# A q projection between two table sums, and value projections beside logits, in a fused attention and state-space kernel

## The chip, the cores and the metric

The kernel runs on one core of a Trainium2 chip. The core has five engines that run side by side and wait for one another through semaphores: TensorE (PE, matrix products, and PEld, its weight loads), VectorE (DVE), ScalarE (ACT), GpSimd (POOL) and SyncE (SP, which here only issues DMA transfers). SP and POOL each issue transfers in order from a queue of their own; the transfers run on 16 DMA engines. TensorE writes into PSUM, a small memory of eight banks, from which ScalarE or VectorE copies results into SBUF, the main on-chip memory. The metric is the device time of one execution in microseconds (us); lower is better.

## The reference

Two independent computations on inputs of 2048 positions and 640 channels, with their results side by side:

```
def _A_ref(x, wqkv, wo):                  # 32 heads of 20, W, dil = 8, 2
    qkv = (x @ wqkv) -> q, k, v
    idx = pos[:, None] - (arange(W) * dil)[None, :];  mask = idx >= 0
    logits = einsum("bhsd,bhswd->bhsw", q, k[idx]) * scale, masked
    o = einsum("bhsw,bhswd->bhsd", softmax(logits), v[idx])
    return o.reshape(B, S, D) @ wo

def _B_ref(u, A_re, A_im, B_re, B_im, C_re, C_im, log_dt, Dskip):
    P = exp(dt * A * l)                   # complex, 640 x 192 x 2048
    K = einsum("dn,dnl,dn->dl", C, P, dt * B).real
    y = irfft(rfft(pad(u)) * rfft(pad(K)))[:L]
    return y + u * Dskip
```

A is attention in which each position sees itself and seven earlier ones, two apart. B makes a convolution kernel K of length 2048 for each channel as a sum over 192 complex exponentials, and convolves the input with it by Fourier transforms of length 4096.

## The kernel before

**Part B.** The 640 channels are worked in five chunks c = 0 to 4 of 128. For a chunk, tables of exponentials and of sines are made (ScalarE) and multiplied into tables P, Q, F, G, X (`small_half`, one half h at a time) and Y (`y_form`, VectorE, line 305). A `unit(c, h, uu)` makes three Y tables and sums them against X with 192 matmuls (`kgen_unit`, lines 318 and 323; TensorE) into Ksb, which four units fill. `transform` is the forward Fourier step of K (two stages of matmuls, lines 337 and 343), `products` multiplies it with the stored transform of u (line 358), `inverse_a` is the first inverse step (line 374): four pieces of 16 matmuls, each copied into Z by ScalarE (line 375); after the fourth piece SP stores Z to Zdram. For chunks 0 to 3 this is interleaved with the next chunk's tables; for chunk 4, `LAST`, it runs beside the attention's second half.

**Part A.** The positions are taken in four strips of 512, each in a first and a second half of 256 (hf = 0, 1). `proj_k`, `proj_q` make k and q transposed, a channel tile ct at a time (10 matmuls and one copy each, lines 464 and 482). `products(hf, w)` multiplies q with k shifted by 2w (VectorE, line 521), `logits(hf, w)` sums that over the 20 channels of each head with a 0/1 matrix Gs (20 matmuls, line 531); `softmax_a`, `softmax_b` follow. The value projection `proj_v(d)` makes a pair of value rows with 40 matmuls into two PSUM banks (line 495), `proj_v1(d)` a single one with 20 into one bank (in the listings under line 420, tile ps_v); `v_halo` fills in the last 14 positions of the strip before. `av_step` multiplies values with the attention weights (VectorE, line 584, into a ring of six buffers) and sums over w on TensorE (ps_o); the positions and channels of it are worked in six groups of eight steps. `out_piece` is the output projection (ps_op).

**The second inverse step.** Class `Inverse`: Z is loaded back in four quarters (`load(qr)`, 15 transfers of 128 KB each, line 637; quarters 0 to 2 are issued before the attention-value groups, quarter 3 between them, part on SP and part on POOL). `part` works three, three or two positions at a time: 24 parts in all, six to a quarter of Z (ps_ib, 8 or 12 matmuls), copied by ScalarE into `ysb` (line 650), a ring of four buffers each of which takes three parts, and stored by SP from there (line 653). `fill(parts)` in the loops hands out the next part. So parts 0 to 5 read the first quarter, 6 to 11 the second, 12 to 17 the third; part 12 uses the ysb buffer of parts 0 to 2 again.

**What sets the order.** The program is written as one stream. A planner gives each engine a fixed order from it before the kernel runs: of the instructions that are ready by its estimates, it takes the one that stands earliest in the program. `keep_in_program_order` and `issue_after` pin some. From `att.in_order()` on, all matmuls of attention and of `part` keep program order. At run time each engine works its list strictly in order.

**Memory.** A pool hands out tiles by tag; a tag has one buffer or `bufs` in rotation, in the order of the program. Rotation sets the order in PSUM too: `big` takes the three two-bank buffers of tag "bank2" (projections of q, k, pairs of v, transform, inverse_a, ps_o), `one` the two one-bank buffers of "bank" (logits, single v, parts, output projection, and `kgen_unit`'s sums). Pool `tabb` holds the tables, laid out in the order P (3 KB a partition), F (4.5), G (6), four Y (6 each), two X (9 each), UD (2), Ksb (4). When it is closed, pool `a1` takes the same place: the pair of product buffers "prod" (20 KB), the pair "v2" (20.5 KB, over most of three Y buffers and the edge of the first X), qT1, lsb1. With `reuse_waits="tile"` a new tile waits until all work on each old tile that it lies over is done.

**Around the change.** For chunk 4 TensorE does, after the first units, `proj_k(0, 0..4)`, unit (4,1,0), unit (4,1,1), and then the five `proj_q(0, ct)` with four products behind each, the logits of the first half with `proj_k(1, ·)` between, `softmax_a(0)`, `proj_q(1, ·)`, and the loop of the second half's logits with `transform(LAST)` at w = 0, `softmax_b(0)` at 2, `products` and the four inverse pieces at 4, and value pairs at w = 1, 3, 5, 7. Eight values are made there as four pairs; the other twelve are made as singles in the first attention-value group, two before each of its first six steps, with two parts at w = 4 and two at w = 5.

Of the kernel before, what the change touches and what calls it, by code (L numbers as in the profile page):

```python
# [402 lines left out]
class Attention:  # L403
# [34 lines left out]
    def open_q0(self):  # L438
        QL = self.ta.tile([128, 9216], bf16, name="ql", tag="R0")
        self.q = [QL[:, 0:5120].rearrange("p (c s i) -> p c s i", c=5, s=4), None]  # L440
        self.lsb[0] = QL[:, 5120:9216].bitcast(f32).rearrange("p (w i) -> p w i", w=W)
        self.wv = self.ta.tile([128, 5, D], bf16, name="wv", tag="TX")
        self.nc.gpsimd.dma_start(out=self.wv[:], in_=self.wsrc[:, :, 2 * D:3 * D])

    def open_rest(self, a1):
        nc = self.nc
# [4 lines left out]
        self.Gs = a1.tile([128, 5, 32], bf16, name="Gs")  # L451
        nc.sync.dma_start(out=self.Gs[:], in_=nc.inline_tensor(gs_np.astype(ml_dtypes.bfloat16), name="c_Gs").ap())
# [55 lines left out]
    def v_halo(self, d0, nd):  # L508
# [8 lines left out]
                MM(ps[to:to + 32], lhsT=self.ident[sl, 0:32], rhs=self.ident[sl, 0:HALO].unsqueeze(1).to_broadcast([32, nd, HALO]), start=True, stop=True, tile_position=(32 * s, to), skip_group_check=True)  # L517
        self.nc.scalar.copy(out=self.v2[:, d0:d0 + nd, 0:HALO], in_=ps)

    def products(self, hf, w, c0=0, c1=5):  # L520
        self.nc.vector.tensor_tensor(out=self.prod[w % (4 - 2 * hf)][:, c0:c1], in0=self.q[hf][:, c0:c1], in1=self.kT[:, hf, c0:c1, :, HALO - DIL * w:HALO - DIL * w + 256], op=A.mult)  # L521

    def logits(self, hf, w):
        nc = self.nc
        MM = self.MM
        if w % 2 == 0:
            self.lps = self.one("ps_l")[:].rearrange("p (a b) -> p a b", a=2)
        ps, pr = self.lps, self.prod[w % (4 - 2 * hf)]
        for ct in range(5):
            for sc in range(4):  # L530
                MM(ps[32 * sc:32 * sc + 32, w % 2], lhsT=self.Gs[:, ct, :], rhs=pr[:, ct, sc, :],
                   start=(ct == 0 and w % 2 == 0), stop=(ct == 4), tile_position=(0, 32 * sc), skip_group_check=True)
        if w % 2 == 1:
            nc.scalar.activation(out=self.lsb[hf][:, w - 1:w + 1, :], in_=ps, func=ACT.Copy, scale=SCALE)
            for ww in (w - 1, w) if hf == 0 else ():
                if ww > 0:
                    nc.gpsimd.memset(self.lsb[0][0:32, ww, 0:DIL * ww], -1e9)
# [121 lines left out]
def body(tc, ctx, pools, prm, B_u, B_Dskip, Sd, Zd, UDd, A_x, A_wqkv, A_wo, out_a, out_b):  # L659
# [37 lines left out]
    def transform(c):  # L697
        Sk[c] = fwd(tc, pools, C, (lambda ut: Kb[c][:, ut, :]), 1, fp)[0]

    def unit(c, h, uu, F, G, X):  # L700
        Ys = [y_form(tc, pools, F, G, uu, k) for k in range(3)]
        kgen_unit(tc, dict(pools, psum=psg), 2 * h + uu, X, Ys, Kb[c])
        if 4 * c + 2 * h + uu in UD_AFTER:
            times_d(tc, pools, C, UDd, *divmod(UD_AFTER.index(4 * c + 2 * h + uu), 2))

    UD_AFTER = [2, 3, 5, 6, 7, 9, 10, 11, 13, 14]
    LAST = NCH - 1
    for c in range(NCH):
# [37 lines left out]
            unit(c, 1, 0, F, G, Xs[0])  # L746
        if c == 0:
            fwd_u(tc, pools, C, Sd, 1)
        unit(c, 1, 1, F, G, Xs[1])
        if c == LAST - 1:  # L750
            att.load_x()
    tabs.close()
    att.open_rest(ctx.enter_context(tc.tile_pool(name="a1", bufs=1, reuse_waits="tile")))
    for ct in range(5):
        att.proj_q(0, ct)
        for w in range(4):
            att.products(0, w, ct, ct + 1)
# [12 lines left out]
    for w in range(W):  # L770
        if w >= 2:
            att.products(1, w)
        att.logits(1, w)
        if w == 0:
            transform(LAST)
        elif w == 2:
            att.softmax_b(0)
        elif w == 4:
            P1, P2, _ = products(tc, pools, Sk[LAST], Sd[LAST], fp, False)
            for f in inverse_a(tc, pools, C, P1, P2, Zd[LAST], fp):  # L780
                f()
        if w in (1, 3, 5, 7):
            att.proj_v(w - 1)
    att.v_halo(0, 8)
    fft.close()
    att.in_order()
# [109 lines left out]
```

## Time and profile before

| what | us |
| --- | --- |
| median of 3 runs | 447.49 (445.54 to 448.25) |
| profiled execution, own time | 445.28 |
| its span | 443.5 |
| TensorE busy, share of the span | 358.7, 81% |
| VectorE busy | 392.6, 89% |
| ScalarE busy | 314.6, 71% |
| mean granted clock of TensorE | 0.915 |

The profile is one execution recorded by the hardware profiler; all its times count from the span's start. A timeline line is: start, duration, engine, line of the program, operation, output <- input with their shapes, count (x), and in brackets the idle time before it and what ended that. A line of engine times by stretch is: from and to, length, then for PE, PEld, DVE, ACT and POOL the busy time with the count, then the granted clock of TensorE (1.00 is full), the share of DMA time, and GB/s. SPq is SP's queue of DMA issues. "issue" is time in which the engine waited for nothing that the profile shows. Matmuls overlap, and their ends are modelled, so the starts are the better guide.

### The profile page before, as it was taken

What the parts mean: (1) busy time and instruction counts of PE and PEld (TensorE: products, weight loads), DVE (VectorE), ACT (ScalarE), POOL (GpSimd) and SP (SyncE); (2) the same over time, 40 slices, a digit from 0 to 9 for tenths busy, and PEclk for the clock granted to TensorE, in tenths of its full rate; (3) what the DMA queues carried; (4) which work ended last, traced back from release to release, by engine and by line L of the source; (5) the groups of instructions that cost most, each with busy time, mean ns of one, the idle gap of its engine ahead of it and who ended that gap; (6) DMA issues with size and microseconds to landing.
All of it is one profiled execution on the core that took longest, in us unless ns stands there. A gap on an engine that the chain in (4) does not pass through costs nothing.

```text
span 443.5 us, 17699 instructions
## 1 busy us (share of the span) xinstructions
PE 358.7 (81%) x8041; PEld 241.5 (54%) x8041; DVE 392.6 (89%) x394; ACT 314.6 (71%) x576; POOL 41.1 (9%) x85
## 2 busy tenths in 40 slices
PE   1385759989878987879687989899997679769896
PEld 0243656867755676457555665544556646424443
DVE  8889999999979999999999889669799989768751
ACT  3984999889998999799997815244486354635653
POOL 7440000000000000000010000000000030503110
PEclk9967888999896999699896989999999699959999
DMA  5589003171251404431299905200004097797243
GB/s 145 185 158 187 5 1 121 38 254 50 96 187 55 98 28 191 143 75 28 120 278 176 248 15 199 98 1 1 1 0 98 2 248 198 196 209 215 82 104 117
DMA packets 45131, 51.62 MB, mean 116 GB/s; under 512 B 31376, under 2 KB 38992, under 8 KB 42368
## 3 DMA queue, kind: packets, MB, share of 16 engines
q1 hardware_dynamic: 41520, 41.41, 35.5%
q0 software_dynamic: 3392, 8.95, 7.2%
q8 instruction: 63, 1.03, 1.0%
q10 hardware_dynamic: 144, 0.12, 0.1%
q14 instruction: 12, 0.10, 0.1%
HBM read 28.03 MB, written 18.35 MB: 105 GB/s over the span
## 4 chain that ended last, share of the span: by engine, by line
PE 44%; ACT 29%; DVE 11%; issue 6%; DMA 5%; SPq 4%; ACTq 0%; POOL 0%; DVEq 0%; POOLq 0%
ACT R L222 10%; ACT A L338 6%; PE ps_k L318 6%; PE ps_ph L247 6%; PE ps_k L323 6%; PE ps_op L420 6%; PE ps_k L464 5%; ACT Sg L344 4%; DVE prod L521 4%; PE ps_ph L250 4%; SPq L637 3%; PE ps_ia L374 3%; DMA Z<-Zdram 3%; PE ps_o L420 3%; PE ps_f L343 2%
## 5 line engine op out<-in xcount | busy, mean ns | idle before, releaser
L305 DVE TENSOR_TENSOR Y<-F,G 128x3072 bf16<-128x3072 bf16 x60 | 103.2, 1759 | 0.4 <-PE ps_k L323 0.3
L222 ACT ACTIVATE R<-LPC 128x192 bf16<-128x192 f32 x225 | 59.3, 359 | 0.1
L247 PE MATMUL ps_ph<-LPC 128*128 128x256 bf16 (+1 forms) x200 | 41.0, 308 | 20.5 <-DMA LPC<-lo 8.0
L318 PE MATMUL ps_k<-Y,X 128*32 128x64 bf16 x1920 | 47.0, 239 | 8.3 <-issue 4.5
L323 PE MATMUL ps_k<-Y,X 64*32 64x64 bf16 x1920 | 43.2, 234 | 2.9 <-issue 2.9
L318 PEld LDWEIGHTS <-X 128*32 128x32 bf16 x1920 | 32.1, 117 | 18.1 <-issue 9.7
L344 ACT CAST Sg<-ps_f 128x1024 bf16<-128x1024 f32 x40 | 37.6, 1025 | 5.8 <-PE ps_f L343 5.8
L338 ACT CAST A<-ps_f 128x1024 bf16<-128x1024 f32 x40 | 37.6, 1032 | 1.6 <-PE ps_f L337 1.4
L584 DVE TENSOR_TENSOR prod<-v,atp 128x2048 bf16<-128x2048 bf16 (+2 forms) x32 | 31.3, 1021 | 8.3 <-PE ps_o L420 5.6
L255 ACT ACTIVATE TX<-ps_ph 128x864 bf16<-128x864 int16 (+1 forms) x40 | 32.3, 864 | 8.2 <-DVE X L271 3.9
L271 DVE TENSOR_TENSOR X<-R,TX 128x1536 bf16<-128x1536 bf16 x40 | 36.5, 958 | 0.0
L343 PE MATMUL ps_f<-A,T 128*128 128x128 bf16 x320 | 23.9, 236 | 14.9 <-ACT A L338 13.5
L323 PEld LDWEIGHTS <-X 64*32 64x32 bf16 x1920 | 29.5, 113 | 11.4 <-issue 4.2
L255 ACT ACTIVATE TA<-ps_ph 128x768 bf16<-128x768 int16 x40 | 30.4, 822 | 2.7 <-PE ps_ph L250 2.4
L247 PEld LDWEIGHTS <-LPC 128*128 128x128 bf16 x200 | 15.1, 102 | 29.0 <-issue 14.1
L343 PEld LDWEIGHTS <-T 128*128 128x128 bf16 x320 | 21.9, 106 | 16.5 <-issue 15.5
L521 DVE TENSOR_TENSOR prod<-ql,kT 128x1024 bf16<-128x1024 bf16 (+1 forms) x24 | 23.1, 1039 | 8.3 <-ACT ql L483 8.3
L250 PE MATMUL ps_ph<-LPC 128*64 128x128 bf16 (+1 forms) x400 | 29.6, 248 | 0.0
L420 PE MATMUL ps_op<-wo,o 128*128 128x320 bf16 x160 | 28.1, 312 | 0.8 <-ACT o L594 0.4
L610 ACT CAST ob<-ps_op 128x320 bf16<-128x320 f32 x28 | 11.9, 431 | 22.1 <-PE ps_op L420 20.4
L375 ACT CAST Z<-ps_ia 128x1024 bf16<-128x1024 f32 x20 | 19.3, 1014 | 11.5 <-PE ps_ia L374 11.5
L374 PE MATMUL ps_ia<-EA,P 128*128 128x128 bf16 x320 | 24.1, 238 | 3.2 <-DVE P L358 3.2
(133 smaller groups left out, 658.8 us busy)
## 6 DMA issues: line engine op xcount, KB each, us to landing
Sdram<-Sg SPq DMA_DIRECT2D x5, 1024.0 KB
P<-Sdram SPq DMA_DIRECT2D x5, 1024.0 KB
P<-Sdram SPq DMA_DIRECT2D x10, 512.0 KB
Zdram<-Z SPq DMA_DIRECT2D x5, 1024.0 KB
Z<-Zdram SPq DMA_DIRECT2D x30, 128.0 KB
U<-in_B_u_dram SPq DMA_DIRECT2D x4, 640.0 KB
UDdram<-UD SPq DMA_DIRECT2D x10, 256.0 KB
out_dram<-ysb SPq DMA_DIRECT2D x32, 80.0 KB
```

Of the source, the lines that this page charges most:

```text
L222: nc.scalar.activation(out=R[:, :, e, :], in_=src, func=ACT.Exp, scale=m)
L247: MM(o[:, :, 0:32], lhsT=L[:, 0:128], rhs=rhs, start=first, stop=last, skip_group_check=True)
L250: MM(o[64 * hh:64 * hh + 64, :, 32:48], lhsT=L[:, 128:192], rhs=rhs[:, :, 16 * hh:16 * hh + 16], start=False, stop=last, skip_group_check= ...
L255: last = nc.scalar.activation(out=dst[:, qs, e0:e0 + 2 * n, :].rearrange("p q (b e) f -> p b e q f", b=2), in_=words.rearrange("p b (e q f ...
L305: nc.vector.tensor_tensor(out=Y[:].rearrange("p q (b a) f -> p q b a f", a=8), in0=fa, in1=gb, op=A.mult)
L318: MM(ps[32 * g:32 * g + 32, t], lhsT=X[:, q, 2 - k, :, f], rhs=Ys[k][:, q, :, f], start=(t == 0 and k == 0), stop=False, tile_position=(0, ...
L323: MM(ps[32 * g:32 * g + 32, t], lhsT=X[hb, q, 2 - k, :, f], rhs=Ys[k][hb, q, :, f], start=False, stop=(k == 2), tile_position=(64 * (g // ...
L338: nc.scalar.copy(out=A1[:, :, 32 * b:32 * b + 32].rearrange("p k (j g) -> p k j g", g=4), in_=ps[:].rearrange("p j k g -> p k j g"))
L343: last = MM(ps[:, kk], lhsT=C["T2"][:, 8 * b + kk, :], rhs=A1[:, 8 * b + kk, :], start=(kk % 4 == 0), stop=True, skip_group_check=True)
L344: nc.scalar.copy(out=Sg[:, :, 8 * b:8 * b + 8, :], in_=ps[:].rearrange("p k (j g) -> p j k g", g=4))
L420: self.MM = lambda *a, **k: self.tc.keep_in_program_order(self.nc.tensor.matmul(*a, **k))
L521: self.nc.vector.tensor_tensor(out=self.prod[w % (4 - 2 * hf)][:, c0:c1], in0=self.q[hf][:, c0:c1], in1=self.kT[:, hf, c0:c1, :, HALO - DI ...
```

## The change

It has three parts.

- The five `proj_q(0, ct)` move into the last unit: after its three Y tables and before its 192 matmuls (`between`). Behind each, VectorE does the products of w = 0 and 1 for this ct alone (`first_products`). Since pool `a1` is not open yet, these ten small products get tiles of `tabb` by tags that are free: P, UD, Ksb, F, G, and one Y. The logits of w = 0 and 1 then follow the unit, before `tabb` is closed. Products 2 to 7 come as whole ones in the loop, and `proj_k(1, ·)` at w = 2 to 6. Gs, which these logits need, moves from `a1` into the tile of wv, and its load with it.
- Six value pairs instead of four are made beside the second half's logits: at w = 1, 2, 3, 4, 5 and 7. The inverse pieces of the last chunk move from w = 4 to behind the pairs of w = 5 (one), behind w = 6 (one) and behind the pair of w = 7 (two).
- The first attention-value group has eight single values instead of twelve, two before each of its first four steps; halos move one step earlier, and parts are handed out as 1, 2, 1, 1 at w = 4, 5, 6, 7 in place of 2, 2 at w = 4, 5.

```diff
-        self.wv = self.ta.tile([128, 5, D], bf16, name="wv", tag="TX")
-        self.nc.gpsimd.dma_start(out=self.wv[:], in_=self.wsrc[:, :, 2 * D:3 * D])
+        WG = self.ta.tile([128, 5 * D + 160], bf16, name="wv", tag="TX")
+        self.wv = WG[:, 0:5 * D].rearrange("p (k c) -> p k c", k=5)
+        self.Gs = WG[:, 5 * D:].rearrange("p (c h) -> p c h", c=5)
+        self.nc.gpsimd.dma_start(out=self.wv, in_=self.wsrc[:, :, 2 * D:3 * D])
...
+    def open_first(self, tabb):
+        tile = lambda n, tag, **k: tabb.tile([128, n, 4, 256], bf16, name="prod0", tag=tag, **k)
+        P, U, K, F, G, Y = tile(1, "P"), tile(1, "UD"), tile(2, "Ksb"), tile(2, "F"), tile(3, "G"), tile(1, "Y", bufs=4)
+        self.first = [[P[:, 0], K[:, 0], F[:, 0], G[:, 0], G[:, 2]], [U[:, 0], K[:, 1], F[:, 1], G[:, 1], Y[:, 0]]]
...
+    def first_products(self, w, ct):
+        self.nc.vector.tensor_tensor(out=self.first[w][ct], in0=self.q[0][:, ct], in1=self.kT[:, 0, ct, :, HALO - DIL * w:HALO - DIL * w + 256], op=A.mult)
...
-    def unit(c, h, uu, F, G, X):
+    def unit(c, h, uu, F, G, X, between=lambda: None):
         Ys = [y_form(tc, pools, F, G, uu, k) for k in range(3)]
+        between()
         kgen_unit(tc, dict(pools, psum=psg), 2 * h + uu, X, Ys, Kb[c])
...
+    def q_first():
+        att.open_first(pools["tabb"])
+        for ct in range(5):
+            att.proj_q(0, ct)
+            for w in range(2):
+                att.first_products(w, ct)
...
-        unit(c, 1, 1, F, G, Xs[1])
+        unit(c, 1, 1, F, G, Xs[1], q_first if c == LAST else lambda: None)
         if c == LAST - 1:
             att.load_x()
+    for w in range(2):
+        att.logits(0, w)
     tabs.close()
     att.open_rest(ctx.enter_context(tc.tile_pool(name="a1", bufs=1, reuse_waits="tile")))
-    for ct in range(5):
-        att.proj_q(0, ct)
-        for w in range(4):
-            att.products(0, w, ct, ct + 1)
-    for w in range(W):
-        if w >= 4:
-            att.products(0, w)
-        att.logits(0, w)
-        if w < 5:
-            att.proj_k(1, w)
+    for w in range(2, W):
+        att.products(0, w)
+        if w < 7:
+            att.proj_k(1, w - 2)
+        att.logits(0, w)
...
-            for f in inverse_a(tc, pools, C, P1, P2, Zd[LAST], fp):
+            ia = inverse_a(tc, pools, C, P1, P2, Zd[LAST], fp)
+        if w > 0 and w != 6:
+            att.proj_v((0, 0, 2, 4, 6, 8, 0, 10)[w])
+        if w >= 5:
+            for f in ia[w - 5:w - 4] if w < 7 else ia[2:]:
                 f()
-        if w in (1, 3, 5, 7):
-            att.proj_v(w - 1)
...
     for w in range(W):
-        if w < 6:
-            att.proj_v1(8 + 2 * w)
-            att.proj_v1(9 + 2 * w)
-            if w in (4, 5):
+        if w < 4:
+            att.proj_v1(12 + 2 * w)
+            att.proj_v1(13 + 2 * w)
+        if w in (3, 4, 5):
+            if w > 3:
                 fill(parts)
-                att.v_halo(*((8, 8) if w == 4 else (16, 4)))
+            if w < 5:
+                att.v_halo(*((8, 8) if w == 3 else (16, 4)))
+            else:
                 fill(parts)
+        if w > 5:
+            fill(parts)
```

More of the change, by code (lines that the diff above doesn't have):

```diff
@@ L441, in open_q0 @@
         self.lsb[0] = QL[:, 5120:9216].bitcast(f32).rearrange("p (w i) -> p w i", w=W)
-        self.wv = self.ta.tile([128, 5, D], bf16, name="wv", tag="TX")
-        self.nc.gpsimd.dma_start(out=self.wv[:], in_=self.wsrc[:, :, 2 * D:3 * D])
-    def open_rest(self, a1):
-        nc = self.nc
+        WG = self.ta.tile([128, 5 * D + 160], bf16, name="wv", tag="TX")
+        self.wv = WG[:, 0:5 * D].rearrange("p (k c) -> p k c", k=5)
+        self.Gs = WG[:, 5 * D:].rearrange("p (c h) -> p c h", c=5)
+        self.nc.gpsimd.dma_start(out=self.wv, in_=self.wsrc[:, :, 2 * D:3 * D])
         gs_np = np.zeros((128, 5, 32), np.float32)
@@ L450, in open_rest @@
                 gs_np[p, ct, (128 * ct + p) // DH] = 1.0
-        self.Gs = a1.tile([128, 5, 32], bf16, name="Gs")
-        nc.sync.dma_start(out=self.Gs[:], in_=nc.inline_tensor(gs_np.astype(ml_dtypes.bfloat16), name="c_Gs").ap())
+        self.nc.sync.dma_start(out=self.Gs, in_=self.nc.inline_tensor(gs_np.astype(ml_dtypes.bfloat16), name="c_Gs").ap())
+    def open_first(self, tabb):
+        tile = lambda n, tag, **k: tabb.tile([128, n, 4, 256], bf16, name="prod0", tag=tag, **k)
+        P, U, K, F, G, Y = tile(1, "P"), tile(1, "UD"), tile(2, "Ksb"), tile(2, "F"), tile(3, "G"), tile(1, "Y", bufs=4)
+        self.first = [[P[:, 0], K[:, 0], F[:, 0], G[:, 0], G[:, 2]], [U[:, 0], K[:, 1], F[:, 1], G[:, 1], Y[:, 0]]]
+    def open_rest(self, a1):
         pairs = [a1.tile([128, 2, 5, 4, 256], bf16, name="prod", tag=t) for t in ("prod", "v2")]
@@ L527, in logits @@
             self.lps = self.one("ps_l")[:].rearrange("p (a b) -> p a b", a=2)
-        ps, pr = self.lps, self.prod[w % (4 - 2 * hf)]
+        ps = self.lps
+        pr = self.first[w] if hf == 0 and w < 2 else [self.prod[w % (4 - 2 * hf)][:, ct] for ct in range(5)]
         for ct in range(5):
             for sc in range(4):
-                MM(ps[32 * sc:32 * sc + 32, w % 2], lhsT=self.Gs[:, ct, :], rhs=pr[:, ct, sc, :],
+                MM(ps[32 * sc:32 * sc + 32, w % 2], lhsT=self.Gs[:, ct, :], rhs=pr[ct][:, sc, :],
                    start=(ct == 0 and w % 2 == 0), stop=(ct == 4), tile_position=(0, 32 * sc), skip_group_check=True)
```

## The prediction

> **What bounds the kernel now.** I read the page first (span and busy shares), then the timelines of VectorE and TensorE from 255 us on, then SP's queue, the clock by stretch, and the DMA rate of 356 to 396 us in forty slices.
>
> ```profile
> span 443.5 us, 17699 instructions
> ...
> PE 358.7 (81%) x8041; PEld 241.5 (54%) x8041; DVE 392.6 (89%) x394; ACT 314.6 (71%) x576; POOL 41.1 (9%) x85
> ```
>
> No engine is full, so each stage has its own limit. VectorE's own gaps, in its timeline:
>
> ```profile
> 275.27 8.65 DVE L305 TENSOR_TENSOR Y<-F,G 128x3072 bf16<-128x3072 bf16 x5
> 292.23 23.07 DVE L521 TENSOR_TENSOR prod<-ql,kT 128x1024 bf16<-128x1024 bf16 x24 [8.31 <-ACT ql L483]
> 317.77 1.23 DVE L541 TENSOR_TENSOR tree<-ql 128x1024 f32<-128x1024 f32 x1 [2.46 <-POOL ql L537]
> ...
> 381.31 3.56 DVE L584 TENSOR_TENSOR prod<-v,atp 128x1536 bf16<-128x1536 bf16 x4 [2.70 <-ACT v L506]
> ```
>
> The 8.31 us before the first product is the gap that the q move aims at; the 2.70 us wait for values is what the pair move aims at. Between 317.8 and 357.3 VectorE waits only 1.7 us in all: that stage is its own. TensorE:
>
> ```profile
> 283.11 0.22 PE L318 MATMUL ps_k<-Y,X 128*32 128x64 bf16 x1 [0.98 <-issue]
> ...
> 286.83 0.23 PE L318 MATMUL ps_k<-Y,X 128*32 128x64 bf16 x1 [1.13 <-issue]
> ...
> 288.77 10.96 PE L482 MATMUL ps_q<-xT,wkq 128*128 128x512 bf16 x50
> ...
> 343.87 0.73 PE L531 MATMUL ps_l<-prod,Gs 128*32 128x256 bf16 x20 [2.19 <-DVE prod L521]
> ...
> 348.28 5.45 PE L374 MATMUL ps_ia<-EA,P 128*128 128x128 bf16 x61 [1.70 <-DVE P L358]
> ...
> 395.28 0.53 PE L420 MATMUL ps_o<-prod,ident 32*32 32x384 bf16 x10 [3.49 <-issue]
> ```
>
> From 268 to 328 us TensorE hardly pauses, so there an order change gives nothing by itself; from 341.3 to 348.3 it is busy 1.6 of 7 us; at 391.8 it stops 3.5 us in mid-step. The DMA rate, one figure per us from 356 to 396, and SP's queue:
>
> ```profile
> GB/s 369 434 299 258 207 234 249 214 231 208 227 217 232 226 195 84 175 206 204 210 192 188 24 193 200 208 160 278 207 241 232 203 224 239 222 268 190 261 224 264
> ```
> ```profile
> 386.52 0.77 SPq L637 DMA_DIRECT2D Z<-UDdram  x1
> 387.59 9.08 SPq L653 DMA_DIRECT2D out_dram<-ysb  x8
> ```
>
> The loads of Z fill this stretch: the last one of the third quarter is issued at 386.52 and, by the completion records of its semaphore, is in at 395.9. Behind it wait the first ysb stores.
>
> **q between the two units.** Before: k projection to 279.1, two units of 4.8 us each (192 matmuls at 19 ns are 3.65, plus the 0.98 and 1.13 pauses), q 10.9, products 292.2 to 315.3. After: unit, q from 283.9 to 294.8, unit to 299.7 (I keep its pause; without it 1.1 earlier), then the first two logits, 0.66 each, to 301.0. VectorE does the ten small products (20 of the same form took 12.1) behind the copies of q, done by about 297. There it stops: the new pair tile "v2" lies over three of the four Y buffers, two read by the last unit and one holding a first product, and a tile in this pool waits for every reader of each tile it covers. So products 2 to 7 start at 301.0, six at 2.75 (four took 11.0): 317.5 against 315.3, a loss of 2.2. What is behind that wait on VectorE: all six products and the softmax tree. Against it: TensorE is free of k by 301.0 + 5 x 2.92 (the period of k plus logits at 304 to 313) = 315.6 and can begin the second q, so VectorE fills part of the 2.46 gap with two small products (1.2), and the 0.75 that it later waited for a logits behind the inverse step goes. 2.2 - 1.2 - 0.75 is +0.3; I take 0 at VectorE's last product (357.3), with bounds -1.2 (no pause in the unit) and +2.2 (nothing fills).
>
> The Gs load moves to SP's queue behind the TX readers (272.9, where POOL's wv load was released too); its successor, the load of P, was issued at 273.65: nothing.
>
> **Value pairs.** Pairs 4 and 6 (2.2 us each) leave 354 to 360 for the 5.4 us of idle TensorE before the inverse step; four single values of pairs 8 and 10 (1.1 each) leave the attention-value stage. The inverse pieces then run beside two pairs instead of alone; the Zdram store stays within 1 us of 354.8. SP's first Z load is held by VectorE's last product, so the stream starts where it did.
>
> **Attention-value group one.** VectorE's work from 358.7 to 378.6 has no gap. With values there it starts at 357.3 and ends at 377.2; the next group starts 4.1 earlier than 381.31. TensorE has 8 single values instead of 12 and paces nothing.
>
> **What is late next.** This decides the sum. Group one hands out 1 + 2 + 1 + 1 = 5 parts, before 2 + 2 = 4; with 8 in group two the thirteenth, part 12, now stands at its end, before group three, on an engine kept in program order. Part 12 needs the third quarter of Z and overwrites the first ysb buffer, whose stores sit on SP behind all 38 loads. Before, it ran at 416, 20 us after its data. Also wv is free at about 366 (eight singles at 1.14 from 357) instead of 380.4, so POOL issues the four wo loads and its six of the fourth quarter then, into the same 16 engines. Bytes are unchanged; only idle DMA time can be won. Slices 15 to 26 of the row above average 157 GB/s, the later ones 230: 12 x 73/230 = 3.8 us. So the third quarter lands at 395.9 - 3.8 = 392.1 (388.5 if POOL's six, 0.56 each, do not get in front; 395.9 if nothing is won). TensorE, ready at about 387 to 389, does part 12 in 0.59 and the first step in 0.54 (the half-clock rows of 387 to 391): 393.2 against 395.74, -2.5. ScalarE's copy of part 12 waits for the stores, near 394; the other PSUM buffer covers that. The last group has one part fewer: -0.3.
>
> **Sum:** 0 - 2.5 - 0.3 = -2.8 us. The profiled execution took 445.28 (span 443.5 and 1.8 around it): 442.5. On the median of the runs shown, 447.49, that is 444.7.
>
> **Clock.** The rows:
>
> ```profile
> 345.40:352.20 6.80, 4.42 (x40) 4.17 (x41) 6.80 (x4) 1.52 (x2) 0.00 (x0) 0.50 0.00 0
> ...
> 386.40:393.20 6.80, 5.19 (x128) 1.90 (x128) 6.80 (x9) 4.01 (x8) 0.55 (x1) 0.50 1.07 226
> ```
>
> After the idle stretch the granted clock is 0.50 and 61 inverse matmuls take 89 ns each, where 34 at 266 us took 61; after the thin work of 380 to 386 it is 0.50 again up to 400. The Trainium skill, "TensorE: Matmul & The Clock Gate", section "Part 1: The HAM clock gate", says that an idle window of about 3.4 us halves the clock and a busy one restores it. By that rule the pairs keep the inverse step at full clock (64 x 28 ns = 1.8 us earlier, off the path here), but group one gets thinner and group two stays at half clock: the rule speaks against pricing group two at full clock, and in rival 1 I do not.
>
> **Rivals.** *1, the Z loads do not hold TensorE* (0.25). They land while group two still runs, as the 20 us of slack before would suggest. Then group two takes its 8.7 us (382.6 to 391.3, half clock) from 378.2, group three starts at 386.9, and the 3.49 pause, whose instruction page was fetched in the full DMA stretch, falls away: up to -8.4 - 0.3. With the quarter in at 388.5 it is -6. I take -6.5: 441.0. Against: the issue pace of SP.
>
> *2, no net gain* (0.20). The wo loads moved to 366 halve SP's stream just when the second quarter is due, and the third lands at 395.9 as before. In the row, loads that landed 0.56 apart alone landed 1.2 apart beside wo. The Trainium skill, "DMA: Bandwidth & Descriptors", section "Queues, rings and completion order", states that an engine takes turns between queues by packet, and the 1.2 agrees. Step one of group three is then done at 395.9 + 0.59 + 0.54 = 397.0, +1.3; less 0.3 that is 448.5.
>
> *3, slower* (0.15): value pairs in front of logits. TensorE's order is fixed beforehand; its 5.4 free us before the inverse step shrink to 1. The second half has two product buffers, so a pair that stands before a logits holds VectorE's product after next by up to 2.2, and everything behind 357 moves with it, SP's first load too. One such wait cancels most of the gain; from two on (4.4) the kernel is slower, with three 447.5 - 2.8 + 6.6 = 451.3. Against: logits go first when ready, and a VectorE product is 2.75 long against 0.66 + 2.2 of TensorE.
>
> **How the numbers follow.** Forecast 0.40 at 444.7. Range 440 to 450.5: rival 1 down to -7.5, rival 3 up to two waits; what is left out is the far end of both. More than 1% (4.5 us) is about what a measurement here tells from no change. Faster by that: rival 1 and the forecast's lower tail (quarter at 388.5 with the start at -1.2), 0.25 + 0.08. Slower by that: 0.12, rival 3 less its single wait. Within: 0.55.
>
> **What would show it.** Right: VectorE's gap near 297 to 301 released by TensorE's logits; product 7 of the first half ending near 317.5; last product near 357; no wait for values near 377; wo issues near 366; a stop of TensorE before part 12, released by a Z load. Wrong: an earlier start of products 2 to 7, waits of VectorE on ps_l between 328 and 357, or group three running at 387.

## The result and the profile after

The changed kernel takes 453.27 us (median of 4 runs, 450.96 to 456.94) against 447.87 for the kernel before on the same chip: a ratio of 1.0132, interval 1.0088 to 1.0176. Predicted were 444.7 and a gain of 2.8 us; by the ratio it is a loss of 5.9. The profiled execution took 453.39, 8.1 us more than that of before.

The page after, span and busy times:

```profile
span 451.6 us, 17688 instructions
...
PE 367.4 (81%) x8041; PEld 245.4 (54%) x8041; DVE 392.6 (87%) x386; ACT 315.2 (70%) x574; POOL 45.4 (10%) x85
```

VectorE does the same 392.6 us as before in a span that is 8.1 us longer, so the loss is waiting. VectorE's timeline (start, busy, engine, line, operation, count, idle ahead of it and what ended it) shows where:

```profile
300.76 16.50 DVE L530 TENSOR_TENSOR prod<-ql,kT 128x5120 bf16<-128x5120 bf16 x6 [3.38 <-PE ps_l L541]
...
349.10 8.29 DVE L530 TENSOR_TENSOR prod<-qT,kT 128x5120 bf16<-128x5120 bf16 x3
...
394.51 1.96 DVE L594 TENSOR_TENSOR prod<-v,atp 128x1536 bf16<-128x1536 bf16 x2 [5.23 <-PE ps_o L420]
```

Up to the last product (349.10 + 8.29 = 357.39; before 357.27) nothing is lost. At 394.5 VectorE waits 5.2 us for TensorE. TensorE's timeline, first the stretch of the inverse step, then the three places where it stands in the attention-value groups:

```profile
351.97 1.26 PE L541 MATMUL ps_l<-prod,wv 128*32 128x256 bf16 x20 [3.95 <-DVE prod L530]
...
354.44 2.10 PE L374 MATMUL ps_ia<-EA,P 128*128 128x128 bf16 x18
356.47 1.26 PE L541 MATMUL ps_l<-prod,wv 128*32 128x256 bf16 x20
357.66 1.09 PE L374 MATMUL ps_ia<-EA,P 128*128 128x128 bf16 x14
...
361.55 1.96 PE L374 MATMUL ps_ia<-EA,P 128*128 128x128 bf16 x32
...
380.79 0.59 PE L420 MATMUL ps_ib<-Z,HB 96*32 96x160 bf16 x12 [4.39 <-DMA Z<-Zdram]
...
393.33 0.59 PE L420 MATMUL ps_ib<-Z,HB 96*32 96x160 bf16 x12 [5.12 <-DMA Z<-Zdram]
...
401.98 0.59 PE L420 MATMUL ps_ib<-Z,HB 96*32 96x160 bf16 x12 [2.87 <-DMA out_dram<-ysb]
```

Two things are to be seen here. The four inverse pieces, which before ran in one go from 346.1 to 353.7, now stand between logits and value pairs in TensorE's fixed order and end at 363.5. And parts 0, 6 and 12, the first parts of the three quarters of Z, each wait for loads: 12.4 us in all, where before only a pause of 3.49 us stood there, in which TensorE waited for nothing that the profile shows. For part 12 the profile names a store, but the last load of its quarter was in at 401.85, 0.13 us ahead of the start. All five kernels that hand out five parts (the changed one and, below, e1, e3, e6 and e10) have the same 0.13 us between this load and part 12, and in e10 the profile names the load itself, so I read it as a wait for the load. The first output projection of group three starts at 402.98 instead of 395.74. What follows it takes 48.6 us, before 47.8.

The loads come late from their beginning. SP's queue and POOL's queue after, from 356 us on:

```profile
357.45 1.25 SPq L647 DMA_DIRECT2D Z<-Zdram  x2
358.75 0.58 SPq L647 DMA_DIRECT2D Z<-UDdram  x1
359.38 0.54 SPq L647 DMA_DIRECT2D Z<-Zdram  x1
364.61 0.34 SPq L377 DMA_DIRECT2D Zdram<-Z  x1
```
```profile
364.11 1.13 POOL L647 DMA_DIRECT2D Z<-Zdram  x2 [45.22 <-PE ps_h L523]
```

SP starts at 357.45 as forecast (357.34 before), but after four loads it stands 4.7 us behind the Zdram store, which goes out 9.8 us later than before. The store and POOL's first load of the first quarter were these lines before:

```profile
354.82 0.33 SPq L377 DMA_DIRECT2D Zdram<-Z  x1
...
354.33 1.13 POOL L637 DMA_DIRECT2D Z<-Zdram  x2 [36.59 <-ACT Z L375]
```

so this load too is 9.8 us late. In between the DMA engines are mostly idle. The two kernels' rows by stretch, before and then after (from and to, length, busy us and count of TensorE, its weight loads, VectorE, ScalarE and GpSimd, then granted clock, DMA share, GB/s):

```profile
356.00:360.00 4.00, 3.77 (x92) 2.73 (x84) 2.51 (x3) 1.61 (x2) 1.66 (x4) 1.00 0.95 340
360.00:364.00 4.00, 2.75 (x48) 1.66 (x45) 3.93 (x4) 1.71 (x3) 0.56 (x1) 1.00 1.06 226
364.00:368.00 4.00, 2.45 (x55) 2.12 (x55) 4.00 (x5) 3.02 (x4) 0.00 (x0) 1.00 1.11 221
```
```profile
356.00:360.00 4.00, 4.00 (x75) 2.90 (x76) 2.52 (x2) 2.02 (x2) 0.00 (x0) 0.75 0.20 58
360.00:364.00 4.00, 4.00 (x77) 3.12 (x73) 2.89 (x4) 2.93 (x4) 0.00 (x0) 1.00 0.26 78
364.00:368.00 4.00, 2.46 (x56) 1.55 (x49) 4.00 (x4) 2.90 (x4) 3.32 (x6) 1.00 0.67 236
```

In these 12 us (340 + 226 + 221) x 4 = 3148 kB moved before, 1488 after. From 368 to 392 us the changed kernel moves 219 to 244 GB/s with the DMA share above 1: the engines are full, and the missing 1660 kB are 7.1 us of transfer at 235 GB/s. In bytes, part of that is made up: the rows from 356 to 392 us add up to 7956 kB before and 7056 after. But wo and POOL's share of the fourth quarter, which go out 4.6 us earlier here (376.33 against 380.95), take part in that; of the Z loads, 20 are in 28.3 us behind P (below) before and 6 after, and 40 us behind P it is 36 and 23.

### The profile page after: what moved, and what is told of

It reads as the page before. It is cut to its first block, busy times and chain, and to the rows that moved or that the text cites. A ratio compares the mean times of both kernels' runs of the same rounds, so it can differ in the third digit from the quotient of the medians.

```text
span 451.6 us, 17688 instructions
## 1 busy us (share of the span) xinstructions
PE 367.4 (81%) x8041; PEld 245.4 (54%) x8041; DVE 392.6 (87%) x386; ACT 315.2 (70%) x574; POOL 45.4 (10%) x85
## 4 chain that ended last, share of the span: by engine, by line
PE 45%; ACT 29%; DVE 9%; DMA 7%; issue 6%; SPq 4%; DVEq 0%; ACTq 0%
ACT R L222 10%; ACT A L338 6%; PE ps_k L318 6%; PE ps_ph L247 6%; PE ps_k L323 6%; PE ps_op L420 6%; DMA Z<-UDdram 4%; PE ps_ph L250 4%; ACT Sg L344 4%; PE ps_q L488 4%; PE ps_f L343 3%; SPq L647 3%; DVE prod L530 3%; ACT Z L375 3%; PE ps_k L470 2%
## 5 line engine op out<-in xcount | busy, mean ns | idle before, releaser
L247 PE MATMUL ps_ph<-LPC 128*128 128x256 bf16 (+1 forms) x200 | 42.6, 317 | 16.0 <-DMA LPC<-lo 8.5
L343 PE MATMUL ps_f<-A,T 128*128 128x128 bf16 x320 | 27.1, 258 | 14.3 <-ACT A L338 13.6
L343 PEld LDWEIGHTS <-T 128*128 128x128 bf16 x320 | 25.3, 119 | 15.6 <-issue 14.3
L250 PE MATMUL ps_ph<-LPC 128*64 128x128 bf16 (+1 forms) x400 | 30.6, 255 | 0.0
L250 PEld LDWEIGHTS <-LPC 128*64 128x64 bf16 x400 | 15.6, 120 | 19.8 <-issue 19.6
L337 PE MATMUL ps_f<-BD,U 128*64 128x128 bf16 x320 | 19.4, 285 | 6.9 <-ACT Z L375 3.4
L358 DVE TENSOR_TENSOR P<-P,Sg 128x4096 bf16<-128x4096 bf16 x10 | 22.8, 2284 | 2.4 <-ACT TA L255 1.4
```

Source lines behind the costliest of these rows:

```text
L247: MM(o[:, :, 0:32], lhsT=L[:, 0:128], rhs=rhs, start=first, stop=last, skip_group_check=True)
L250: MM(o[64 * hh:64 * hh + 64, :, 32:48], lhsT=L[:, 128:192], rhs=rhs[:, :, 16 * hh:16 * hh + 16], start=False, stop=last, skip_group_check= ...
L343: last = MM(ps[:, kk], lhsT=C["T2"][:, 8 * b + kk, :], rhs=A1[:, 8 * b + kk, :], start=(kk % 4 == 0), stop=True, skip_group_check=True)
```

## The experiments

Below, P is the start of VectorE's two P products (343.74 before, 344.69 after); times from P leave out what happened earlier in an execution. "Loads in" counts the Z loads complete 28.3 us behind P, by their completion records. Ratios are against the kernel before, run beside each group, and rest on 4 to 10 executions of a kernel; the two right columns are of the one traced execution, which is long for e7 (450.22, median 444.36) and short for e5 (449.03, median 450.85).

| kernel | ratio, 95% interval | loads in | P to first output projection |
|---|---|---|---|
| before | 1 | 20 | 52.0 |
| changed | 1.0132 [1.0088, 1.0176] | 6 | 58.3 |
| e1 | 1.0028 [0.9995, 1.0060] | 18 | 53.4 |
| e2 | 1.0050 [1.0011, 1.0089] | 17 | 53.8 |
| e3 | 1.0102 [1.0060, 1.0143] | 9 | 57.1 |
| e4 | 1.0008 [0.9970, 1.0047] | 13 | 52.7 |
| e5 | 1.0112 [1.0067, 1.0157] | 10 | 53.6 |
| e6 | 1.0042 [1.0007, 1.0077] | 17 | 52.0 |
| e7 | 0.9941 [0.9904, 0.9979] | 20 | 50.8 |
| e8 | 0.9992 [0.9956, 1.0029] | 17 | 50.7 |
| e9 | 0.9928 [0.9880, 0.9975] | 17 | 49.1 |
| e12 | 0.9920 [0.9878, 0.9962] | 20 | 47.4 |
| e13 | 1.0039 [0.9998, 1.0080] | 8 | 56.1 |
| e14 | 1.0027 [0.9994, 1.0060] | 14 | 53.9 |

**Splitting the change.** First the inverse pieces back in their place, then each half of the change alone, then the late pieces alone.

```diff
 # e1, against the changed kernel
-            ia = inverse_a(tc, pools, C, P1, P2, Zd[LAST], fp)
+            for f in inverse_a(tc, pools, C, P1, P2, Zd[LAST], fp):
+                f()
         if w > 0 and w != 6:
             att.proj_v((0, 0, 2, 4, 6, 8, 0, 10)[w])
-        if w >= 5:
-            for f in ia[w - 5:w - 4] if w < 7 else ia[2:]:
-                f()
```

> The changed kernel with all four pieces of the last inverse step handed to the planner together again, right behind their two products and ahead of the fourth value pair, as the kernel before does; q between the units, the six pairs and the new placing of the parts stay. Theory A, the late Zdram store: in the changed kernel the pieces stood behind value pairs and logits in TensorE's fixed order, the store went out at 364.6 us instead of 354.8, and all Z loads behind it came late. Then here the store is issued at 355 +- 1.5, the first quarter of Z is in by 370 (changed kernel: 380), TensorE's stops before parts 0 and 6 (4.4 and 5.1 us) are gone, group three starts 5 to 8 us earlier than its 403, and the time is 445 to 448. Theory B, the thirteenth part: part 12 at the end of group two waits for the first ysb buffer's stores behind all loads on SP; its stop of about 3 us stays and the time stays above 449.5. Theory C, the q move: the time stays at 452 to 454, since q is unchanged here.

Measured: 448.85 against 447.49. Of the loss of 1.3%, 1.0% is gone, and the stops before parts 0 and 6 with it (0.3 and none). The stop before part 12 is not, as theory B had it: TensorE waits 5.52 us there, and the time is just above the 445 to 448 of theory A. So the late pieces carry most of the loss, and what is left, 1.3 us above the kernel before (by the interval -0.2 to +2.7) where 2.8 below was forecast, has other causes.

```diff
 # e2, against the kernel before; open_first, first_products, q_first, Gs and logits as in the change
-        unit(c, 1, 1, F, G, Xs[1])
+        unit(c, 1, 1, F, G, Xs[1], q_first if c == LAST else lambda: None)
...
+    for w in range(2):
+        att.logits(0, w)
     tabs.close()
...
-    for w in range(W):
-        if w >= 4:
-            att.products(0, w)
+    for w in range(2, W):
+        att.products(0, w)
+        if w < 7:
+            att.proj_k(1, w - 2)
         att.logits(0, w)
-        if w < 5:
-            att.proj_k(1, w)
```

> The kernel before with only q's first half between the two units (with its first products and logits); value pairs, inverse pieces and parts as before. Theory A (the late store): the time of the kernel before, 446 to 449, and the store at 355 +- 1; VectorE's last product stays near 357.3. Theory B (the thirteenth part): the same. Theory C (the q move costs): 451 to 454.

Measured: 449.46, +0.5%. Not free, and not the 451 to 454 of theory C. VectorE's timeline of e2, the wait for the first logits and the one ahead of its last product:

```profile
303.62 16.50 DVE L530 TENSOR_TENSOR prod<-ql,kT 128x5120 bf16<-128x5120 bf16 x6 [3.36 <-PE ps_l L541]
...
359.01 2.82 DVE L530 TENSOR_TENSOR prod<-qT,kT 128x5120 bf16<-128x5120 bf16 x1 [1.50 <-PE ps_l L541]
```

From the start of the last matmuls of k's projection to P it is 65.7 us here and 64.9 before, +0.8; and the wait ahead of the last product is 1.50 instead of 0.75, since the whole inverse step still stands before that product's logits. Together 1.6, near the 2.0 measured.

```diff
 # e3, against the kernel before: the edit of e4, below, group one of the change, and
-        if w in (1, 3, 5, 7):
-            att.proj_v(w - 1)
+        if w > 0 and w != 6:
+            att.proj_v((0, 0, 2, 4, 6, 8, 0, 10)[w])
 # e4, against the kernel before
-            for f in inverse_a(tc, pools, C, P1, P2, Zd[LAST], fp):
-                f()
+            ia = inverse_a(tc, pools, C, P1, P2, Zd[LAST], fp)
         if w in (1, 3, 5, 7):
             att.proj_v(w - 1)
+        if w >= 5:
+            for f in ia[w - 5:w - 4] if w < 7 else ia[2:]:
+                f()
```

> The kernel before with only the second half of the change: six value pairs, the pieces of the inverse step spread over the last three logits, and the new placing of the parts; q as before. Theory A (the late store): the store at 362 to 366, Z loads late, 451.5 to 454.5. Theory B (the thirteenth part): the same time, but with a stop of 3 us or more at part 12 and a first quarter that does not hold TensorE. Theory C (the q move): 446 to 449.

> The kernel before with one edit: the four pieces of the inverse step are handed over one at a time behind the fifth, one behind the sixth and two behind the last logits, as in the changed kernel. Four value pairs, parts and q as before. Theory A (the late store alone costs it): the store is issued at 360 to 364 instead of 354.8 and the time rises by 0.6 us for each us of that, as in the changed kernel (5.8 for 9.8): 450.5 to 453. Theory B or C: the time of the kernel before, 446.5 to 449, since parts and q are untouched. If the late store costs only together with six pairs, which free VectorE for group two earlier, it is between: 448.5 to 450.5.

Measured: e3 452.87 with the store 19.1 us behind P, as theory A had it (before 11.1, changed 19.9); e4 448.57, no loss, with the store 15.0 behind P. The planner's order explains the difference: with four pairs the pieces end 4 us later than before, with six 8. Four cost nothing, since the loads of the first quarter had some 5 us to spare ahead of part 0, which was this line before:

```profile
376.25 0.38 PE L420 MATMUL ps_ib<-Z,HB 96*32 96x160 bf16 x12
```

By their completion records, taken in the program's order, the last of them was in at 371.1 or a little earlier before, and in e4 at 374.47, 1 us ahead of part 0 at 375.44. In the changed kernel it was in at 380.65, 36.0 us behind P instead of 27.4, and part 0 stood 4.39 us for it. The rate of 0.6 us per us that I had put in e4's expectation was wrong: it is slack first, then a wait.

**Part 12 and the order of the inverse step.**

```diff
 # e5: the changed kernel with four parts in group one (e7 and e8 have this too)
-        if w > 5:
+        if w == 7:
             fill(parts)
 # e6: the kernel before with six pairs, group one of the changed kernel, and
         elif w == 4:
             P1, P2, _ = products(tc, pools, Sk[LAST], Sd[LAST], fp, False)
             for f in inverse_a(tc, pools, C, P1, P2, Zd[LAST], fp):
                 f()
-        if w in (1, 3, 5, 7):
-            att.proj_v(w - 1)
+        if w > 0 and w != 4:
+            att.proj_v((0, 0, 2, 4, 0, 6, 8, 10)[w])
 # e7: e6 with four parts in group one;  e8: e7 with q between the units
```

> The changed kernel with one edit: the attention-value group one hands out four parts of the out-projection of the inverse step instead of five (none at its seventh step), so that part 12 leaves group two. Theory B (part 12 holds TensorE at the end of group two): its stop of 2.9 us goes, group three starts 2 to 3 us earlier and the time is 450 to 451.5. Theory A (the late store, the loads of the first two quarters): the stops before parts 0 and 6 stay (4.4 and 5.1 us) and the time falls by no more than 1 us from 453.3: 452.3 to 454.

> The kernel before with six value pairs, but the inverse step as before: pairs 0, 2 and 4 behind the second, third and fourth logits, then the four pieces together behind their products, then pair 6 behind the sixth logits and 8 and 10 behind the last two; the parts of the changed kernel (five in group one); q as before. Theory A+B: the store is at 355 +- 1.5 and the first two quarters hold nothing; logits six is not behind a pair, so VectorE's last product does not wait more than 1 us; but the wo loads, which come 4 us earlier, take the engines' time in front of the third quarter, which is in at 395 to 397, and part 12 at the end of group two stops TensorE for 3 to 6 us: 446.5 to 449.5. Theory A alone (nothing but the order of the inverse step): 443 to 446.

> The same as the run before it with four parts in group one, so that part 12 is not in group two but comes after group three, as in the kernel before. Theory A+B: no stop at the end of group two; it ends 3 to 4 us earlier than in the kernel before: 443 to 445.5. If part 12's wait only passes to the next thing that is late (wo for the first output projection, or half-clock thin work in group two): 446 to 448.

> The same as the run before it with q's first half between the last two units, as in the changed kernel: the change with both repairs. Theory C2, from the run with q alone (+2 us): VectorE's wait of 3.4 us for the first two logits costs 1 to 2 us here too, 445 to 447.5. If what q alone cost was only noise of the units' pauses: as the run before, within 0.7 us.

Measured: e5 450.85 (+1.1%), e6 449.06 (+0.4%), e7 444.36 (-0.6%), e8 445.73 (-0.1%), against 446.48. In e5 part 12's stop is gone, those before parts 0 and 6 stay (4.09 and 5.17), and the ratio falls by only 0.2%. What part 12 costs behind a late stream is not settled by that: the two intervals allow a fall of up to 0.8%, the median of 450.85 lies in theory B's range and the ratio in theory A's, and in the traces the first output projection comes 4.7 us earlier behind P. Where the stream is in time part 12 decides the sign: e6 and e7 differ in that part alone, and in 1.0%. TensorE in e6:

```profile
394.71 0.74 PE L420 MATMUL ps_ib<-Z,HB 96*32 96x160 bf16 x12 [5.31 <-DMA out_dram<-ysb]
```

Part 12's own input, the third quarter, is in at 394.58, the same 0.13 us earlier; the profile names a store that ended about then. e8 repeats the price of q beside e7: +0.5%.

**What about the late pieces costs time?** Theory A said the late store. So e9 keeps e7's order on TensorE and holds only the store; e13 holds the memory under the first quarter of Z as well.

```diff
 # e9, against e7: the store leaves inverse_a's last piece and is issued here
     att.v_halo(0, 8)
+    nc.scalar.copy(out=held[0][:, 127, 31:32], in_=att.v2[:, 0, 0:1])
+    held[1]()            # the Zdram store; held[0] is the tile Z it reads
 # e13, against e9: three more copies between these two lines
+    for t in (P1[:, 31, 31, 3:4], P2[:, 31, 31, 3:4], EA[:, 1, 127:128]):
+        nc.scalar.copy(out=held[0][:, 127, 31:32], in_=t)
```

> The kernel of e7_v_order_p4 (q as before, six pairs, the inverse step in its old place, four parts in group one) with one thing added: the Zdram store is held back by the data. It is issued behind the halo copies of the values, and a copy of one element of v into the last column of Z makes it wait for them (so one column of the last inverse step is overwritten). TensorE's order stays as in e7. Theory A (the late store costs it by the Z stream alone): the store goes out 18 to 20 us after VectorE's P products begin (e7: 10.8; the changed kernel: 19.9), TensorE stops before parts 0 and 6 as in the changed kernel, and the time is 4 to 6 us above e7's: 448.5 to 450.5. Theory A2 (the fixed order of TensorE costs it, with logits and softmax behind the pieces, and the stream has slack): within 1.5 us of e7, 444 to 446.

> The kernel of e9_late_store with the memory under the first quarter of Z held as well: behind the copy that holds the store, three more one-column copies read the last elements of P1, P2 and EA into the same column of Z, so that the tile of the first quarter, which lies over them, is free only after the halo copies (again one column of the last inverse step is overwritten). TensorE's order is that of e7 and e9. Theory E (in the changed kernel the loads of the first quarter were held by the memory that the late inverse pieces read; 5 loads were in by 368 us against 12 in the kernel before): POOL's six loads go out 18 to 20 us after the P products begin (e9: 10.2, changed kernel: 19.4), the stops before parts 0 and 6 come to 3 to 5 us each, and the time is 3 to 6 us above e9's: 447.5 to 450. Theory A2 (TensorE's own order, with the softmax behind it, costs it): within 1 us of e9, 443.5 to 445.5.

Measured: e9 444.10 against 447.44, -0.7%, level with e7, although its store goes out 19.3 us behind P, nearly as late as in the changed kernel. Theory A falls: the store's lateness alone costs nothing there. What e9 does not test is a long stand of SP: it has six loads ahead of the store and stands 1.65 us behind it, the changed kernel four loads and 4.7 us (e5 2.5, e13 2.7, with losses of the same size). e13 449.82 against 447.85, +0.4%: 1.1% above e9, with POOL's loads 21.7 us behind P instead of 10.2 (19.4 in the changed kernel). TensorE in e9 and in e13, at parts 0 and 6:

```profile
378.37 0.39 PE L421 MATMUL ps_ib<-Z,HB 96*32 96x160 bf16 x12 [1.14 <-DMA Z<-Zdram]
...
385.26 0.59 PE L421 MATMUL ps_ib<-Z,HB 96*32 96x160 bf16 x12 [0.49 <-DMA Z<-UDdram]
```
```profile
383.12 0.59 PE L421 MATMUL ps_ib<-Z,HB 96*32 96x160 bf16 x12 [7.10 <-DMA Z<-Zdram]
...
393.71 0.59 PE L421 MATMUL ps_ib<-Z,HB 96*32 96x160 bf16 x12 [2.85 <-DMA Z<-UDdram]
```

and the first two stretches of the DMA, again e9, then e13:

```profile
356.00:360.00 4.00, 4.00 (x100) 3.00 (x94) 3.29 (x3) 2.51 (x4) 3.32 (x6) 1.00 0.46 122
360.00:364.00 4.00, 4.00 (x88) 2.64 (x80) 2.02 (x2) 1.51 (x2) 0.00 (x0) 1.00 0.74 199
```
```profile
356.00:360.00 4.00, 4.00 (x90) 2.84 (x85) 3.41 (x2) 1.21 (x2) 0.00 (x0) 1.00 0.08 21
360.00:364.00 4.00, 4.00 (x88) 2.75 (x81) 2.17 (x3) 2.59 (x4) 0.00 (x0) 1.00 0.55 167
```

POOL's first loads in the two:

```profile
356.45 1.13 POOL L638 DMA_DIRECT2D Z<-Zdram  x2 [36.18 <-DVE prod L522]
```
```profile
365.64 1.13 POOL L638 DMA_DIRECT2D Z<-Zdram  x2 [47.74 <-PE ps_v L421]
```

In e9 POOL's six loads of the first quarter go out from 356.45 on, 0.60 us after the last matmul of the pieces; in e13 from 365.64 on, 0.29 us after the last of the added copies, which ends at 365.35. The 0.60 us is the same in the kernel before, the changed kernel and e1 to e12, wherever the pieces end (from 353.64 in e12 to 363.51 in the changed kernel); the names that the profile gives for these waits change from run to run, the distance does not. That is theory E: the first quarter's tile lies over what the inverse step reads, and the loads of Z that need nothing of this step (all of the first quarter's 15 but the two that read the last chunk's Zdram) are held by it all the same. In e13 TensorE's order is that of e9, so the order itself is not needed for a loss of this kind and size. Some 3.8 us of what e13's trace has more than e9's lie behind the first output projection (50.6 us to the end, 46.8 in e9), where nothing was edited.

The reverse test takes the loads out from under the late pieces, by exchanging two buffers:

```diff
 # e14, against e5; e15 does the same to e12
-        pool, tag = ((self.a2, "Z"), (self.att.ta, "LPC"), (self.att.a1, "prod"), (self.att.ta, "U"))[qr]
+        pool, tag = ((self.att.ta, "LPC"), (self.a2, "Z"), (self.att.a1, "prod"), (self.att.ta, "U"))[qr]
```

> The kernel of e5_a_p4 (the changed kernel with four parts in group one, inverse pieces late) with the buffers of the first and second quarter of Z exchanged: the first quarter goes into the long free buffer, the second into the one that lies over the inverse step's tiles. Theory E: the first quarter's loads, but for the three of the last chunk, go out before the pieces end, on SP and POOL from 358 on; the stop before part 0 shrinks from 4.1 to under 1.5 us and the stop before part 6 by 2 or more, and the time falls from 450.9 to 446 to 448.5. Theory A2: within 1 us of e5, 450 to 452.

> The kernel of e12_pair_first (the fastest so far, q as before, inverse pieces in their old place) with the same exchange of buffers. Theory E: the first quarter's loads were not held there and nothing waits for them, so no more than 1 us either way: 442.5 to 444.5.

Measured: e14 449.05, +0.3%, 0.8% under e5 by the ratios. Its trace supports only half of it. The first quarter is free of the hold: POOL's first load goes out 4.3 us before the pieces end, and the stop before part 0 is gone (0.38). But part 6 now waits 10.76 us for the second quarter, which took over the held memory; and SP stands 5.6 us at a load that waits for the store's landing. 40 us behind P, 24 loads are in, as in e5, and the first output projection is not earlier. Exchanging buffers moves the hold, so this run does not settle theory E from its side. The time lies between what the two theories had. e15 is 0.7% under the kernel before (444.81 against 447.85), level with e12 and 0.3 us above the expected range.

**The wo loads and a pair in front of a logits.**

```diff
 # e10, against e6, and e11, against e7
-            nc.gpsimd.dma_start(out=self.wo[32 * dd:32 * dd + 32], in_=wsrc[dd])
+            nc.sync.dma_start(out=self.wo[32 * dd:32 * dd + 32], in_=wsrc[dd])
 # e12, against e7
-        if w > 0 and w != 4:
-            att.proj_v((0, 0, 2, 4, 0, 6, 8, 10)[w])
+        if w > 0 and w != 6:
+            att.proj_v((0, 0, 2, 4, 6, 8, 0, 10)[w])
```

> The kernel of e6_v_order (part 12 at the end of group two) with the four wo loads on SP's queue behind the loads of the first three quarters of Z, instead of on POOL's queue, where they go out as soon as wv is free. Theory D (wo and POOL's part of the fourth quarter share the DMA engines with the third quarter, which is why it was in no earlier): the third quarter is in 2 to 3 us earlier, part 12's stop of 5.3 us shrinks by that, and the time falls from 449.1 to 446 to 447.5. If POOL's loads of the fourth quarter, which then go out earlier still, take wo's place: 448 to 449.5. If wo comes too late for the first output projection in group three: a new stop before ps_op and 449 or more.

> The same edit of the wo loads on the kernel of e7_v_order_p4, where part 12 comes after group three and nothing in group two waits for the third quarter. Theory D: no gain there, since no part waits: within 1 us of e7's 444.4, or up to 2 us above it if the output projection waits for wo.

> The kernel of e7_v_order_p4 with the fourth value pair ahead of the sixth logits again (handed over behind the fifth, as the changed kernel does), so that TensorE's order is inverse step, pair, logits. The price of one pair in front of a logits, by the prediction up to 2.2 us: VectorE's last product waits 2 to 3.5 us for that logits instead of 0.5 to 1.5, and the time is 1.5 to 2.5 us above e7's: 446 to 447. If the slack behind it takes the wait: within 0.7 us of e7.

Measured: e10 446.56 against 447.44 (0.9970, 0.9925 to 1.0015), 0.7% under e6; e11 445.44 (0.9939), level with e7; e12 443.45 (0.9920). With wo behind the third quarter, that quarter is in 48.3 us behind P in e11 and 48.8 in e10, against 50.7 in e6 and 52.1 in e7: theory D holds for its 2 to 4 us, and in e10, where part 12 waits for that quarter, it shows in the time. In e11 TensorE then waits 5.47 us for wo ahead of the output projection, and nothing is won. In e12 VectorE's last product does wait longer:

```profile
356.56 2.83 DVE L521 TENSOR_TENSOR prod<-qT,kT 128x5120 bf16<-128x5120 bf16 x1 [2.41 <-PE ps_l L531]
```

2.41 us, in e7 0.43, but the softmax behind it starts 16.7 us after P in e12 and 16.8 in e7, because e7 has a pair between the last two logits instead. A pair must stand somewhere; before which of these two logits made no difference. e12, the changed kernel's six pairs with q and inverse step as before and part 12 out of group two, is the fastest version: 0.8% under the kernel before (0.4 to 1.2).

## Why the prediction was wrong

**The step that failed** is "the Zdram store stays within 1 us of 354.8. SP's first Z load is held by VectorE's last product, so the stream starts where it did". The store went out at 364.61. The second sentence is right of SP alone; POOL's six loads, which the step did not follow, started at 364.11 instead of 354.33. The step priced the spread pieces by their TensorE time and did not ask what is held until the last of them has read its operands. Measured price: 0.6 to 1.2%, 3 to 5 us (the changed kernel against e1 1.0%, e3 against e6 0.6%, e5 against e8 1.2%, and the hold alone, e13 against e9, 1.1%). The store, which the step did name, is not what costs (e9).

**q between the units**: the forecast of each event held (wait near 297 ended by logits, product seven of the first half done at 317.3 against 317.5, last product 357.39 against 357.3). That last figure was right by luck, by a loss and a gain: P starts 0.9 us later, and the spread pieces spared the wait ahead of the last product. With the pieces in their place q costs 0.5% (e2, e8), 2 us where 0 was taken; the upper bound was +2.2.

**Value pairs**: they fill 2 of the 5.4 us that TensorE was idle before the inverse step (3.3 are left in e7 and e12), and with everything else in place the six pairs are worth 0.6 to 0.8% (e7, e12), 2.6 to 3.6 us, what had been forecast for the whole change.

**What is late next**: that part 12 would gate group three was right. Its size was not. The 3.8 us do not come out of their own row: slices 15 to 26 average 170 GB/s, not 157, so it should have been 3.1. The third quarter was forecast 3.8 us earlier, at 48.4 behind P; it was in at 50.7 in e6, 52.1 in e1 and 57.2 in the changed kernel (52.2 before). wo went out at 376 in e6 and in the changed kernel, not at 366, since the single values that free wv are handed out with the steps of the group and end at 376; it then sat in front of the third quarter. That is rival 2's mechanism, and e1, the change with its inverse step in time, came out at +1.3 us where rival 2 had +1.0; that the two are so close is chance, since e1 also bears the price of q. A wait for values near 377 was to be gone; one of 1.51 us stands at 382. Rival 1, loads that hold nothing, was the farthest off.

**Rival 3** had the slower side with the wrong price: the pair in front of a logits cost nothing in e12, and the last product was not late. Pairs and logits in front of the inverse pieces were the harm.

**Clock.** The row of the late pieces, after:

```profile
351.20:358.00 6.80, 6.03 (x73) 4.02 (x73) 6.80 (x4) 2.63 (x3) 0.00 (x0) 0.50 0.00 0
```

The Trainium skill, "TensorE: Matmul & The Clock Gate", section "Part 1: The HAM clock gate", lets the clock fall after an idle window of about 3.4 us. The trace agrees: TensorE, which the pairs left dry after 348.0, stood 3.95 us for the next product, and the half clock follows. So my step "the pairs keep the inverse step at full clock" failed too; group two at half clock, as forecast, did come (0.50 from 380 on), here behind the stop of 4.39 us, but in e1 and e12 from about 383 on without one.

## What to carry to other kernels

When a step is moved, list not only its instructions and outputs but the memory it reads: whatever is loaded into that memory next is held until its last reader is done, on every queue that loads there. Price a later producer by slack first (4 us cost nothing here, 8 cost 3 to 5), and where a load stream then runs at a full rate, count the kilobytes not moved in the gap. When the number of pieces handed out ahead of a boundary changes by one, look what the piece that crosses it needs.

## What the runs showed of the hardware that I had not expected

The changed kernel does not make up the gap at the start of its Z stream: 14 loads fewer at 28.3 us behind P are still 13 fewer at 40. In e4 most of a smaller gap is made up (7 fewer, then 3: 13 against 20, 33 against 36). The kernel before had stretches of 149 to 199 GB/s with a DMA share of 0.5 to 0.8 (368 to 380 us) to spare; the changed kernel had none between 368 and 392 us.

The time behind the first output projection is not constant for unchanged work. It is 46.8 to 47.8 us in ten of the seventeen traces (the kernel before, e2, e4, e5, e8, e9, e11, e12, e14 and e15), and 48.6 to 50.6 in the other seven (the changed kernel, e1, e3, e6, e7, e10 and e13). The granted clock from 425 to 435 us is 1.00 in each of the ten and 0.66 to 0.80 in each of the seven. Some 1 to 3 us go with it. All five kernels with five parts in group one are among the seven; e7 and e13, with four, are too. What calls up this second spell of half clock, some 20 us behind the first one, stays open.
